# Whole TensorE tiles for the last block of tokens, and a new order of work, in a kernel of linear attention followed by a mixture of attention experts

## The chip, the cores and the metric

The kernel runs on one core of a Trainium2 chip. The metric is device time in microseconds of one execution of the whole program. A core has a matrix engine (TensorE, PE; its weight loads are shown apart as PEld), a vector engine (VectorE, DVE), an activation engine (ScalarE, ACT), a general engine (GpSimd, POOL) and a queue that issues the transfers (SyncE, SP). Each works through its own instructions in the order in which the program gives them and waits for the others by semaphores. PE writes into PSUM, small banks that DVE or ACT empty into SBUF.

## The reference

B = 8 batches of S = 576 tokens, 8 heads of 64 (D = 512), E = 4 experts of width 64, the best 2 of 4 per token. All inputs are f32.

```python
kv  = einsum('bhsd,bhse->bhde', k, v)          # linear attention
out = einsum('bhsd,bhde->bhse', q, kv)
x   = out / sqrt(mean(out * out, -1) + 1e-06) * g_norm
logits = x @ w_gate                            # the best 2 of 4 experts, softmax weights w
for e in range(E):                             # causal attention in each expert
    qe, ke, ve = x @ wq[e], x @ wk[e], x @ wv[e]
    a  = softmax(causal(qe @ ke.T / 8))
    ye = a @ ve @ wo[e]
    result += (e chosen by the token) * w_e * ye
```

## The kernel before

**Tiling.** 576 tokens are cut into NB = 5 blocks: four of 128 and one of REM = 64. D = 512 is cut into NCH = 4 chunks of 128 rows. The four experts go as EP = 2 pairs, two experts side by side on the 128 partitions.

**Steps of one batch, b.** `lk`, `lv`, `lr`, `lq` load k, v, the last 64 tokens of both, and q. `kv` (L409) makes the 64x64 products per head. `q` (L437) transposes q block by block on PE, `qc` (L440) copies it to the tile qT. `out` (L474) multiplies each block of qT by the k-v tile, to which the gate's logits are appended; `oc`, `sq`, `red` copy, square and sum; `nw` is a Newton iteration for the inverse root on DVE; `xm` scales on GpSimd into an x tile (a pool of six, which the stages of the weights share). `x` and `xc` (L560, L563) transpose it to xT. `m8` to `gate` make the expert weights. `v` (L611), `qp` and `kp` (L629) project. For each pair: `sc` (L654) makes five pieces of transposed scores, `exp` (L668) writes them as bf16 into PT, in which key block kb has a strip of the queries from kb's first token on (576, 448, 320, 192 and 64 wide), `msk` masks the diagonal on GpSimd. `pv` (L686) multiplies PT by v with a column of ones: bank 0 holds query blocks 0 to 2 (12 matmuls), bank 1 blocks 3 and 4 (18). `rc`, `iv`, `oc2` (L713 to L726) take the inverse of the ones' column, multiply it by the gate and scale. They read blocks 0 to 2 together, then block 3, then block 4, which has 64 rows. `ot` (L733) transposes five blocks, `otc` copies them to OT, `y` (L743) multiplies by wo, `yc` and `st` copy and store.

**Where block 4 is short.** In `out`, `v`, `y` its stationary operand has 64 columns; in `pv` the stationary operand of query block 4 has 64 columns, and for key block 4 it has 64 rows as well; in `ot` the input has 64 rows. The profile writes the part of PE that is used as rows*columns: 128*128, 128*64, 64*64, 64*128. The `kv` step uses 128*64 by design, two heads beside one another, and the transposes of block 4 of q and x are 64*128.

**Order.** `graph` (L22) lists every step with its engine, its time on the engine, a latency, its needs and the buffers that it holds. `urgency` (L161) gives each a due time from the tables OFFSET, STEP, SECOND (pair 1 against pair 0) and PERIOD (one batch against the next). `plan` (L176) walks through time and always starts the step that can start first, of equals the one due first. The order found is the program's order on every engine, the SP queue's among them. A step that waits holds up all behind it on its engine. The pools' sizes are in POOLS (L142): qT 1, xT 2, PT 3, OT 2, sm and bg (PSUM) 2 and 3, x 6.

Of the kernel before, what the change touches and what calls it, by code (L numbers as in the profile page):

```python
# [21 lines left out]
def graph(B):  # L22
# [18 lines left out]
    for b in range(B):  # L41
        for p in R4 if b == 0 else R2:
            w = 1.0 if b == 0 else 2.0
            tl = (("k", b), ("v", b))
            add(("lk", b, p), "SP", 0.5, 0.45 * w, [("kv", b - 2, c) for c in R4] if p == 0 else [], tl[:1])
            add(("lv", b, p), "SP", 0.5, 0.45 * w, [("kv", b - 2, c) for c in R4] if p == 0 else [], tl[1:])
            if p == 0:
                add(("lr", b), "SP", 1.2, 1.2, [("kv", b - 2, c) for c in R4])
        for i in R5:
            add(("lq", b, i), "SP", 1.1, 1.2 if i < NF else 0.6, [], (("q", b),))  # L50
        if b == 0:
            add(("lg0",), "SP", 2.5, 0.2)
# [22 lines left out]
        for i in R5:  # L75
            pe(("out", b, i), 0.93, [("qc", b, i), ("kvx", b), ("kgc", b)], (("bg", "out", b, i), ("qT", b)))
# [28 lines left out]
        for i in R5:  # L105
            pe(("v", b, i), 0.47, [("xc", b, i), ("ws", "v", 0), ("ws", "v", 1)], (("sm", "v", b, i), ("xT", b)))
            dve(("vc", b, i), 0.43, [("v", b, i)] + [("pv", b - 2, p, g) for p in R2 for g in R2], (("sm", "v", b, i),))
        for p in R2:
            for nm in "qk":
                pe((nm + "p", b, p), 1.06, xT + [("ws", nm, 0), ("ws", nm, 1)], (("bg", nm, b, p), ("xT", b)))  # L110
# [15 lines left out]
            for g in range(3):
                nd = [("pv", b, p, min(g, 1)), ("gate", b)]
                tl = (("bg", "pv", b, p), ("osc", b, p), ("gate", b))
                dve(("rc", b, p, g), 0.17, nd[:1], tl[:2])
                dve(("iv", b, p, g), 0.17, [("rc", b, p, g), ("gate", b)], tl[1:])  # L130
                dve(("oc2", b, p, g), 0.56 if g == 0 else 0.29, [("iv", b, p, g)], tl[:2])
            pe(("ot", b, p), 0.28, [("oc2", b, p, g) for g in range(3)], (("sm", "ot", b, p), ("osc", b, p)))
            act(("otc", b, p), 0.64, [("ot", b, p)], (("sm", "ot", b, p), ("OT", b)))
        for i in R5:
            pe(("y", b, i), 0.45, [("otc", b, 0), ("otc", b, 1), ("wo", "o", 0), ("wo", "o", 1)], (("sm", "y", b, i), ("OT", b)))
# [5 lines left out]
NF = 4  # L141
POOLS = {  # L142
    "k": 2, "v": 2, "q": 2, "sm": 2, "bg": 3, "qT": 1, "kvT": 2, "gl": 2, "x": 6, "xT": 2, "gate": 2,
    "qTp": 3, "PT": 3, "osc": 2, "inv": 2, "OT": 2, "y": 4,
}
PERIOD = 25.7
OFFSET = dict(
    lk=-101.2, lv=-101.2, lr=-101.2, lq=-86.0, lg0=-200, wg=-60, lw=-35.8, ws=-10.8, lwo=-85, wo=-30,
    kv=-61.6, kvx=-60.6, kvc=-60.6, q=-57.9, qc=-75.4, kt=-138.5, ktc=-138.5, kg=-137.5, kgc=-137.5,
    out=-27.6, oc=112.9, sq=29.9, red=-136.3, nw=93.2, gl=94.2, lg=95.2, xm=24.8, x=-29.3, xc=-80.7,  # L150
    m8=19.2, sh=19.2, ex=19.2, mk=19.2, gt=19.2, den=19.2, rd=19.2, gate=19.2, v=2.0, vc=-91.6, qp=40.7,
    qpc=12.5, kp=35.4, kpc=7.2, sc=-1.2, exp=-49.5, msk=4.3, pv=-109.0, rc=-99.4, iv=-99.4, oc2=-99.4,
    ot=13.9, otc=13.9, y=26.5, yc=-17.4, st=26.5,
)
# [21 lines left out]
def plan(tasks, pools, prio):  # L176
# [15 lines left out]
    while len(order) < len(tasks):  # L192
# [42 lines left out]
def kernel(  # L235
# [74 lines left out]
    nc.gpsimd.memset(zrow[:], 0.0)  # L310
    for j in range(2):
# [4 lines left out]
        nc.gpsimd.memset(t[:, :, :, Hd : Hd + 1], 1.0)  # L316
        vexts.append(t)
# [156 lines left out]
    def out_mm(b, i):  # L474
        t0, nt = blocks[i]
# [135 lines left out]
    def v_mm(b, i):  # L611
        t0, nt = blocks[i]
# [16 lines left out]
    def proj(nm, b, pr):  # L629
        p_p = big(nm, b, pr)  # L630
        for c in range(NCH):
            for s in range(2):
# [3 lines left out]
                    rhs=tiles["xT", b][:, c, s * HALF : (s + 1) * HALF],  # L636
# [31 lines left out]
    def exp(b, pr, j):  # L668
        PT = buf(("PT", b, pr), [P, 2, strips], BF16, "PT")
# [132 lines left out]
```

## Time and profile before

| | us |
|---|---|
| median of 3 runs (lowest, highest) | 285.91 (283.67, 286.38) |
| profiled execution | 285.5 |
| its span, first to last instruction | 283.4 |
| PE busy, share of the span | 252.3, 89% |
| DVE busy | 184.7, 65% |
| ACT busy | 160.0, 56% |
| POOL busy | 76.5, 27% |

Busy time is the union of an engine's instructions. Matmuls are pipelined, and an instruction's duration contains time in which the next one runs already; what a group costs in a busy stretch is read from its start to the start of the next group. The granted clock is the share of TensorE's full speed that a stretch had.

### The profile page before, as it was taken

What the parts mean: (1) busy time and instruction counts of PE and PEld (TensorE: products, weight loads), DVE (VectorE), ACT (ScalarE), POOL (GpSimd) and SP (SyncE); (2) the same over time, 40 slices, a digit from 0 to 9 for tenths busy, and PEclk for the clock granted to TensorE, in tenths of its full rate; (3) what the DMA queues carried; (4) which work ended last, traced back from release to release, by engine and by line L of the source; (5) the groups of instructions that cost most, each with busy time, mean ns of one, the idle gap of its engine ahead of it and who ended that gap; (6) DMA issues with size and microseconds to landing.
All of it is one profiled execution on the core that took longest, in us unless ns stands there. A gap on an engine that the chain in (4) does not pass through costs nothing.

```text
span 283.4 us, 6610 instructions
## 1 busy us (share of the span) xinstructions
PE 252.3 (89%) x2576; PEld 219.6 (77%) x2576; DVE 184.7 (65%) x554; ACT 160.0 (56%) x281; POOL 76.5 (27%) x146
## 2 busy tenths in 40 slices
PE   0479768898999797999999999899999999999984
PEld 0469667687898686899889988798889987888850
DVE  1436885988979886266877588857695788215140
ACT  0021203545365568548673977277757777895953
POOL 7000032107107108302072205420271018211210
PEclk9999968999999999799999999999999999999997
DMA  1999998999899951089325962000210111031224
GB/s 42 299 253 307 170 252 217 205 273 262 280 197 230 271 169 56 2 244 222 109 95 130 293 156 85 11 2 37 81 54 0 39 74 58 0 114 57 72 97 168
DMA packets 75551, 40.28 MB, mean 142 GB/s; under 512 B 54272, under 2 KB 70656, under 8 KB 75520
## 3 DMA queue, kind: packets, MB, share of 16 engines
q1 hardware_dynamic: 75520, 39.86, 55.1%
q8 instruction: 20, 0.33, 0.5%
q14 instruction: 11, 0.09, 0.1%
HBM read 30.42 MB, written 9.44 MB: 141 GB/s over the span
## 4 chain that ended last, share of the span: by engine, by line
PE 70%; DVE 14%; DMA 6%; SPq 5%; ACT 2%; issue 2%; ACTq 0%; DVEq 0%
PE p_out L478 12%; PE p_sc L659 9%; PE p_pv L695 7%; PE p_y L747 7%; PE p_k L633 6%; PE p_v L615 6%; PE p_q L633 6%; PE p_q L433 5%; PE p_kv L415 5%; PE p_x L433 4%; SPq L352 3%; DMA w_stage<-in_moe_wq_dram 2%; DMA w_stage<-in_moe_wv_dram 2%; DVE inv L719 2%; DVE mk L588 2%; DVE osc L726 2%
## 5 line engine op out<-in xcount | busy, mean ns | idle before, releaser
L679 POOL TENSOR_SCALAR_AFFINE_SELECT PT<-PT 128x256 bf16<-128x256 bf16 (+1 forms) x80 | 30.1, 387 | 153.1 <-ACT PT L673 139.5
L673 ACT ACTIVATE PT<-p_sc 128x576 bf16<-128x576 f32 (+3 forms) x80 | 51.6, 711 | 9.0 <-PE p_sc L659 8.7
L553 POOL TENSOR_TENSOR x_tok<-o_sb,rs 128x512 f32<-128x512 f32 (+1 forms) x40 | 41.8, 1061 | 40.7 <-DVE rs L529 33.1
L478 PE MATMUL p_out<-kvx,qT 128*128 128x136 f32 (+1 forms) x320 | 47.8, 298 | 1.8 <-DVE qT L443 0.9
L478 PEld LDWEIGHTS p_out<-kvx,qT 128*128 128x128 f32 (+1 forms) x320 | 42.6, 194 | 3.7 <-DVE qT L443 1.1
L659 PE MATMUL p_sc<-qTp,kT 128*128 128x288 f32 (+2 forms) x192 | 39.2, 325 | 0.5 <-ACT PT L673 0.5
L488 DVE COPY o_sb<-p_out 128x544 f32<-128x544 f32 (+1 forms) x40 | 28.4, 717 | 16.9 <-PE p_out L478 15.5
L494 ACT ACTIVATE sq<-o_sb 128x512 f32<-128x512 f32 (+1 forms) x40 | 25.3, 635 | 21.5 <-DVE o_sb L488 20.1
L659 PEld LDWEIGHTS p_sc<-qTp,kT 128*128 128x128 f32 x192 | 28.8, 195 | 5.4 <-issue 1.6
L415 PE MATMUL p_kv<-v_b,k_b 128*64 128x64 f32 x512 | 22.7, 238 | 9.9 <-DMA k_b<-in_k_dram 9.6
L415 PEld LDWEIGHTS p_kv<-v_b,k_b 128*64 128x64 f32 x512 | 19.5, 149 | 12.1 <-DMA v_b<-in_v_dram 9.5
L443 DVE COPY qT<-p_q 128x512 f32<-128x512 f32 (+1 forms) x40 | 25.1, 635 | 5.4 <-PE p_q L433 4.5
L566 ACT CAST xT<-p_x 128x512 fp32r<-128x512 f32 (+1 forms) x40 | 21.4, 544 | 12.7 <-PE p_x L433 12.4
L500 DVE TENSOR_REDUCE ms<-sq 128x8 f32<-128x520 f32 (+1 forms) x40 | 27.2, 685 | 1.8 <-ACT sq L494 1.3
L695 PE MATMUL p_pv<-vext,PT 128*128 128x65 bf16 (+2 forms) x480 | 25.8, 196 | 3.0 <-DVE osc L726 3.0
L695 PEld LDWEIGHTS <-PT 128*128 128x128 bf16 (+2 forms) x480 | 21.5, 101 | 8.8 <-issue 3.1
L754 ACT COPY y<-p_y 128x512 f32<-128x512 f32 (+1 forms) x40 | 23.1, 595 | 9.1 <-PE p_y L747 6.9
L615 PE MATMUL p_v<-wv_r,xT 128*128 128x256 f32 (+1 forms) x160 | 26.2, 293 | 1.3 <-DVE wv_r L395 0.8
L625 DVE CAST vext<-p_v 128x256 bf16<-128x256 f32 (+1 forms) x40 | 16.7, 420 | 16.2 <-PE p_v L615 16.0
L433 PE MATMUL p_q<-ident_f,q_b 128*128 128x128 f32 (+1 forms) x160 | 25.7, 291 | 1.5 <-ACT xT L566 1.2
L648 ACT CAST kT<-p_k 64x576 fp32r<-64x576 f32 x32 | 20.3, 635 | 11.1 <-PE p_k L633 10.9
L747 PE MATMUL p_y<-wo_b,OT 128*128 128x512 bf16 (+1 forms) x80 | 25.0, 405 | 0.5 <-ACT OT L741 0.4
(67 smaller groups left out, 348.3 us busy)
## 6 DMA issues: line engine op xcount, KB each, us to landing
q_b<-in_q_dram SPq DMA_DIRECT2D x32, 256.0 KB, 5.6
out_dram<-y SPq DMA_DIRECT2D x32, 256.0 KB, 2.0
v_b<-in_v_dram SPq DMA_DIRECT2D x14, 512.0 KB, 7.4
k_b<-in_k_dram SPq DMA_DIRECT2D x14, 512.0 KB, 6.3
v_b<-in_v_dram SPq DMA_DIRECT2D x4, 256.0 KB, 4.2
k_b<-in_k_dram SPq DMA_DIRECT2D x4, 256.0 KB, 4.4
k_rem<-in_k_dram SPq DMA_DIRECT2D x8, 128.0 KB, 6.3
v_rem<-in_v_dram SPq DMA_DIRECT2D x8, 128.0 KB, 6.5
```

The costliest lines, as they stand in the source:

```text
L415: nc.tensor.matmul(p_kv[hh * Dh : (hh + 1) * Dh, c, :], lhsT=lhs, rhs=rhs, start=(j == 0), stop=(j == NF), skip_group_check=True,)
L433: nc.tensor.transpose(p_t[:, c, :nt], src[:nt, 2 * c : 2 * c + 2, :].rearrange("p h d -> p (h d)"), ident_f[:nt, :nt])
L478: nc.tensor.matmul(p_o[:nt, c // 2, (c % 2) * 2 * GW : (c % 2 + 1) * 2 * GW], lhsT=tiles["qT", b][:, c, t0 : t0 + nt], rhs=kvx[b % 2][:, c ...
L488: nc.vector.tensor_copy(out=ob[:nt, i].rearrange("p (k h) g -> p k (h g)", k=2), in_=big("out", b, i)[:nt, :, 0 : 4 * GW])
L553: nc.gpsimd.tensor_tensor(out=buf(("x", b, i), [P, H, Dh], FP32, "x_tok")[:nt], in0=ob[:nt, i, :, 0:Dh], in1=st["rstd", b][:nt, i * H : (i ...
L615: nc.tensor.matmul(p_v[:nt, :], lhsT=tiles["xT", b][:, c, t0 : t0 + nt], rhs=w_r["v"][:, c, :, :].rearrange("p e f -> p (e f)"), start=(c ...
L633: nc.tensor.matmul(p_p[:, s, 0:HALF], lhsT=w_r[nm][:, c, 2 * pr : 2 * pr + 2, :].rearrange("p e f -> p (e f)"), rhs=tiles["xT", b][:, c, s ...
L659: nc.tensor.matmul(p_s[:, el, o : o + hi - lo], lhsT=kTs[pr][el][:, kb * P : (kb + 1) * P], rhs=tiles["qTp", b, pr][:, lo:hi], start=True, ...
L673: nc.scalar.activation(PT[:, :, d0 : d0 + o], big("sc", b, pr, j)[:, :, 0:o], ACTF.Exp, scale=scale)
L679: nc.gpsimd.affine_select(out=d, in_=d, compare_op=AluOpType.is_ge, fill=0.0, base=0, pattern=[[0, 2], [1, w]], channel_multiplier=-1,)
L695: nc.tensor.matmul(p_O[:nq, bank, (2 * n + el) * (Hd + 1) : (2 * n + el + 1) * (Hd + 1)], lhsT=PT[:nk, el, col : col + nq], rhs=vexts[b % ...
L747: nc.tensor.matmul(p_y[:nq, :], lhsT=tiles["OT", b][:, pr, s0 : s0 + nq], rhs=wo_b[:, pr, :], start=(pr == 0), stop=(pr == EP - 1),)
```

## The change

The whole last block is made 128 wide. qT, xT, PT and OT, until now buffers from pools, become constant tiles with 64 more columns at the end, set to zero once: one qT, two xT and OT, three PT. In them chunk c's block 4 is read 128 wide, so it reaches over the first 64 tokens of the next chunk or strip; the 64 output rows that come of it are never stored. The rows of v that block 4 lacks are set to zero, its column of ones too. So `out`, `v`, `pv`, `ot` and `y` work on 128*128 tiles throughout; the transposes of block 4 of q and x and the `kv` step stay as they are. With all rows present, `rc`, `iv`, `oc2` read blocks 3 and 4 together: two reads a pair where there were three. One exponential of a column of zeros is put ahead of everything on ACT.

In the planner the needs that the pools expressed are written out, the times of many steps are set anew, the SP queue's latency too, and all of OFFSET, STEP, SECOND and PERIOD. Among the due times, the q, k and v weights (`lw`) move from -35.8 to -50.6, ahead of k and v of batch 2 (2 x 25.4 - 101.1 = -50.3); and the two transfers of wo (-82) come behind the first q block of batch 0 where they came behind the third.

```diff
-            add(("lk", b, p), "SP", 0.5, 0.45 * w, [("kv", b - 2, c) for c in R4] if p == 0 else [], tl[:1])
+            add(("lk", b, p), "SP", 0.5, 0.5 * w, [("kv", b - 2, c) for c in R4] if p == 0 else [], tl[:1])
...
-            add(("lq", b, i), "SP", 1.1, 1.2 if i < NF else 0.6, [], (("q", b),))
+            add(("lq", b, i), "SP", 0.7, 1.35 if i < NF else 0.7, [], (("q", b),))
...
-                    add(("lw", nm, p), "SP", 1.0, 1.3, (), (("x", nm, p),))
+                    add(("lw", nm, p), "SP", 1.0, 1.5, (), (("x", nm, p),))
...
-            pe(("kv", b, c), 0.88, [("lk", b, piece), ("lv", b, piece), ("lr", b)], (("sm", "kv", b), ("k", b), ("v", b)))
+            pe(("kv", b, c), 0.82, [("lk", b, piece), ("lv", b, piece), ("lr", b)], (("sm", "kv", b), ("k", b), ("v", b)))
...
+                ("qc", b, i), 0.42 if last else 0.69, [("q", b, i), ("out", b - 1, i), ("out", b - 1, NF)],
...
-            pe(("out", b, i), 0.93, [("qc", b, i), ("kvx", b), ("kgc", b)], (("bg", "out", b, i), ("qT", b)))
+            pe(
+                ("out", b, i), 0.95, [("qc", b, i), ("qc", b, 0), ("kvx", b), ("kgc", b)],
+                (("bg", "out", b, i),),
+            )
...
+                [("x", b, i)] + [("v", b - 2, j) for j in R5] + [(m, b - 2, p) for m in ("qp", "kp") for p in R2],
...
-            hold = (0.25, 0.25, 0.39, 0.28, 0.29)
+            hold = (0.27, 0.27, 0.43, 0.33, 0.45)
...
+            old = [("pv", n // 2, n % 2, g) for g in R2]
...
+                act(("exp", b, p, j), took[j], [("sc", b, p, j)] + old, (("bg", "sc", b, p, j),))
...
-            for g in range(3):
+            for g in R2:
...
-PERIOD = 25.7
+PERIOD = 25.4
 OFFSET = dict(
-    lk=-101.2, lv=-101.2, lr=-101.2, lq=-86.0, lg0=-200, wg=-60, lw=-35.8, ws=-10.8, lwo=-85, wo=-30,
-    kv=-61.6, kvx=-60.6, kvc=-60.6, q=-57.9, qc=-75.4, kt=-138.5, ktc=-138.5, kg=-137.5, kgc=-137.5,
-    out=-27.6, oc=112.9, sq=29.9, red=-136.3, nw=93.2, gl=94.2, lg=95.2, xm=24.8, x=-29.3, xc=-80.7,
+    lk=-101.1, lv=-101.1, lr=-101.1, lq=-83.0, lg0=-200, wg=-60, lw=-50.6, ws=-25.6, lwo=-85, wo=-30,
+    kv=-61.7, kvx=-60.7, kvc=-60.7, q=-60.4, qc=-50.3, kt=-108.9, ktc=-108.9, kg=-107.9, kgc=-107.9,
+    out=-44.7, oc=31.8, sq=45.8, red=-155.3, nw=62.4, gl=63.4, lg=64.4, xm=93.6, x=-27.6, xc=-100.1,
...
-    x=1.5, xc=2.0, out=1.9, oc=1.9, sq=1.9, red=1.9, v=0.9, vc=0.5, y=1.7, yc=2.0, st=1.6, lq=1.5,
+    x=0.4, xc=0.4, out=1.4, oc=1.4, sq=1.5, red=1.4, v=0.9, vc=1.0, y=1.1, yc=1.1, st=1.1, lq=1.8,
...
-SECOND = 9.2
+SECOND = 15.6
...
+    warm = const.tile([P, 1], FP32, name="warm")
+    nc.scalar.activation(warm[:], zrow[:, 0:1], ACTF.Exp)
+
+    PAD = NB * P - S
+    qT = const.tile([P, NCH * S + PAD], FP32, name="qT")
+    nc.gpsimd.memset(qT[:, NCH * S :], 0.0)
...
+        t = const.tile([P, NCH * S + PAD], FP32R, name=f"xT{j}")
+        nc.vector.tensor_copy(out=t[:, NCH * S :], in_=zrow[:, 0:PAD])
...
+        t = const.tile([P, 2, strips + PAD], BF16, name=f"PT{j}")
+        nc.gpsimd.memset(t[:, :, strips:], 0.0)
...
+    def blocks_of(t, c):
+
+        return t[:, c * S : c * S + NB * P]
...
+        nc.gpsimd.memset(t[REM:P, NF], 0.0)
         vexts.append(t)
...
-                p_o[:nt, c // 2, (c % 2) * 2 * GW : (c % 2 + 1) * 2 * GW],
-                lhsT=tiles["qT", b][:, c, t0 : t0 + nt],
+                p_o[:, c // 2, (c % 2) * 2 * GW : (c % 2 + 1) * 2 * GW],
+                lhsT=blocks_of(qT, c)[:, i * P : (i + 1) * P],
...
-                p_v[:nt, :],
-                lhsT=tiles["xT", b][:, c, t0 : t0 + nt],
+                p_v[:],
+                lhsT=blocks_of(xTs[b % 2], c)[:, i * P : (i + 1) * P],
...
-                    nk = blocks[kb][1]
-                    col = strip_off[kb] + s0 - kb * P
+                    col = strip_off[kb] + (qc - kb) * P
                     nc.tensor.matmul(
-                        p_O[:nq, bank, (2 * n + el) * (Hd + 1) : (2 * n + el + 1) * (Hd + 1)],
-                        lhsT=PT[:nk, el, col : col + nq],
-                        rhs=vexts[b % 2][:nk, kb, 2 * pr + el, :],
+                        p_O[:, bank, (2 * n + el) * (Hd + 1) : (2 * n + el + 1) * (Hd + 1)],
+                        lhsT=PT[:, el, col : col + P],
+                        rhs=vexts[b % 2][:, kb, 2 * pr + el, :],
...
-    PARTS = ((0, 0, 3), (3, 1, 1), (4, 1, 1))
...
-                p_t[:, s0 : s0 + nq], tiles["osc", b, pr][:nq, qc, :, :].rearrange("p e f -> p (e f)"), ident_b[:nq, :nq]
+                p_t[:, qc * P : (qc + 1) * P], tiles["osc", b, pr][:, qc, :, :].rearrange("p e f -> p (e f)"), ident_b[:]
...
-                p_y[:nq, :], lhsT=tiles["OT", b][:, pr, s0 : s0 + nq], rhs=wo_b[:, pr, :],
+                p_y[:], lhsT=blocks_of(OTs[b % 2], pr)[:, qc * P : (qc + 1) * P], rhs=wo_b[:, pr, :],
```

## Rows read from the trace of the kernel before

**Rows 1.** The page: span, then busy us (share) and instructions of each engine

```profile
span 283.4 us, 6610 instructions
PE 252.3 (89%) x2576; PEld 219.6 (77%) x2576; DVE 184.7 (65%) x554; ACT 160.0 (56%) x281; POOL 76.5 (27%) x146
```

**Rows 2.** Stretches: length, PE, PEld, DVE, ACT, POOL busy (instructions), PE clock, DMA share, GB/s

```profile
22.00:35.00 13.00, 11.86 (x136) 10.88 (x134) 9.81 (x20) 3.16 (x5) 0.00 (x0) 1.00 1.04 241
35.00:68.00 33.00, 26.63 (x241) 23.91 (x242) 26.02 (x78) 12.01 (x22) 7.94 (x10) 0.90 1.01 246
68.00:130.00 62.00, 57.85 (x622) 51.18 (x621) 46.83 (x137) 37.22 (x67) 21.15 (x34) 0.97 0.76 183
130.00:265.00 135.00, 133.26 (x1379) 118.07 (x1378) 90.88 (x285) 95.25 (x168) 39.91 (x72) 1.00 0.29 81
```

**Rows 3.** Timeline of PE around P@V: start, us, engine, line, operation, form, count

```profile
203.30 1.54 PE L695 MATMUL p_pv<-vext,PT 128*128 128x65 bf16 x30
204.78 0.62 PE L747 MATMUL p_y<-wo_b,OT 128*64 128x512 bf16 x2
...
209.21 0.54 PE L695 MATMUL p_pv<-vext,PT 128*128 128x65 bf16 x12
209.68 0.69 PE L415 MATMUL p_kv<-v_b,k_b 128*64 128x64 f32 x16
...
210.95 1.18 PE L695 MATMUL p_pv<-vext,PT 128*128 128x65 bf16 x18
212.06 1.32 PE L633 MATMUL p_q<-xT,wq_r 128*128 128x288 f32 x8
```

**Rows 4.** The same timeline around v, y, ot and out

```profile
201.38 1.11 PE L615 MATMUL p_v<-wv_r,xT 128*128 128x256 f32 x8
202.33 0.69 PE L659 MATMUL p_sc<-qTp,kT 128*128 128x288 f32 x4
202.86 0.60 PE L747 MATMUL p_y<-wo_b,OT 128*128 128x512 bf16 x2
...
205.32 0.97 PE L659 MATMUL p_sc<-qTp,kT 128*128 128x448 f32 x4
...
218.90 0.52 PE L736 MATMUL p_ot<-ident_b,osc 128*128 128x128 bf16 x5
219.35 1.19 PE L478 MATMUL p_out<-kvx,qT 128*128 128x136 f32 x8
...
220.81 1.09 PE L478 MATMUL p_out<-kvx,qT 128*128 128x136 f32 x8
221.74 0.60 PE L433 MATMUL p_x<-ident_f,x_tok 128*128 128x128 f32 x4
...
225.86 1.14 PE L478 MATMUL p_out<-kvx,qT 128*64 128x136 f32 x8
226.94 0.61 PE L747 MATMUL p_y<-wo_b,OT 128*128 128x512 bf16 x2
```

**Rows 5.** Weight loads by line and form: count, busy us, mean ns, idle before

```profile
L478 PEld LDWEIGHTS p_out<-kvx,qT 128*128 128x128 f32 x256 | 35.5, 209 | 1.8 <-DVE osc L726 0.9 <-PE p_out L478 0.4
L695 PEld LDWEIGHTS <-PT 128*128 128x128 bf16 x320 | 11.8, 97 | 5.9 <-issue 3.1 <-POOL PT L679 0.8
L478 PEld LDWEIGHTS p_out<-kvx,qT 128*64 128x64 f32 x64 | 7.1, 136 | 1.9 <-DVE qT L443 1.1 <-issue 0.4
```

**Rows 6.** Chain that ended last, in order of time: start, us, what

```profile
17.50 1.28 ACT L427
...
58.98 5.69 DMA w_stage<-in_moe_wv_dram
...
140.65 1.04 PE p_k L633 x8
...
170.11 1.04 PE p_k L633 x8
```

**Rows 7.** Timeline of the SP queue: start, us, line, transfer, count

```profile
40.92 5.00 SPq L392 DMA_DIRECT2D w_stage<-in_moe_wq_dram  x4
```

More of the change, by code (lines that the diff above doesn't have):

```diff
@@ L215, in plan @@
         if eng == "SP":
-            dma = max(dma, t + hold + 1.3) + lat
-            fin = dma + 0.5
+            dma = max(dma, t + hold + 1.6) + lat
+            fin = dma + 0.6
         end = max(end, fin)
@@ L310, with tokens @@
     nc.gpsimd.memset(zrow[:], 0.0)
+    warm = const.tile([P, 1], FP32, name="warm")
[3 more added lines that the diff above has]
+    nc.gpsimd.memset(qT[:, NCH * S :], 0.0)
+    xTs, PTs, OTs = [], [], []
+    for j in range(2):
+        t = const.tile([P, NCH * S + PAD], FP32R, name=f"xT{j}")
+        nc.vector.tensor_copy(out=t[:, NCH * S :], in_=zrow[:, 0:PAD])
+        xTs.append(t)
+        t = const.tile([P, EP * S + PAD], BF16, name=f"OT{j}")
+        nc.gpsimd.memset(t[:, EP * S :], 0.0)
+        OTs.append(t)
+    for j in range(3):
+        t = const.tile([P, 2, strips + PAD], BF16, name=f"PT{j}")
+        nc.gpsimd.memset(t[:, :, strips:], 0.0)
+        PTs.append(t)
+    def blocks_of(t, c):
+        return t[:, c * S : c * S + NB * P]
+    def tokens(t, i):
+        t0, nt = blocks[i]
+        return t[:, 0 : (t.shape[1] - PAD)].rearrange("p (c s) -> p c s", s=S)[:, :, t0 : t0 + nt]
     for j in range(2):
@@ L440, in q_copy @@
     def q_copy(b, i):
-        t0, nt = blocks[i]
-        qT = buf(("qT", b), [P, NCH, S], FP32, "qT")
-        nc.vector.tensor_copy(out=qT[:, :, t0 : t0 + nt], in_=small(None, "q", b, i)[:, :, :nt])
+        nt = blocks[i][1]
+        nc.vector.tensor_copy(out=tokens(qT, i), in_=small(None, "q", b, i)[:, :, :nt])
     def kt(b):
@@ L474, in out_mm @@
     def out_mm(b, i):
-        t0, nt = blocks[i]
         p_o = big("out", b, i)
@@ L563, in x_copy @@
     def x_copy(b, i):
-        t0, nt = blocks[i]
-        xT = buf(("xT", b), [P, NCH, S], FP32R, "xT")
-        nc.scalar.copy(xT[:, :, t0 : t0 + nt], small(None, "x", b, i)[:, :, :nt])
+        nt = blocks[i][1]
+        nc.scalar.copy(tokens(xTs[b % 2], i), small(None, "x", b, i)[:, :, :nt])
     def small_t(b, name, shape):
@@ L635, in proj @@
                     lhsT=w_r[nm][:, c, 2 * pr : 2 * pr + 2, :].rearrange("p e f -> p (e f)"),
-                    rhs=tiles["xT", b][:, c, s * HALF : (s + 1) * HALF],
+                    rhs=blocks_of(xTs[b % 2], c)[:, s * HALF : (s + 1) * HALF],
                     start=(c == 0),
@@ L677, in msk @@
             w = blocks[kb][1]
-            d = tiles["PT", b, pr][:w, :, strip_off[kb] : strip_off[kb] + w]
+            d = PTs[(2 * b + pr) % 3][:w, :, strip_off[kb] : strip_off[kb] + w]
             nc.gpsimd.affine_select(
@@ L701, in pv @@
                     )
-    PARTS = ((0, 0, 3), (3, 1, 1), (4, 1, 1))
     def part(b, pr, g):
-        qc, bank, n = PARTS[g]
-        nq = blocks[qc][1]
-        o = (qc - GROUPS[bank][1][0]) * 2 * (Hd + 1)
-        po = big("pv", b, pr)[:nq, bank, o : o + n * 2 * (Hd + 1)].rearrange("p (n f) -> p n f", f=Hd + 1)
-        iv = buf(("inv", b, pr), [P, NB, 2], FP32, "inv")[:nq, qc : qc + n, :]
-        return qc, n, nq, po, iv
+        bank, qcs = GROUPS[g]
+        qc, n = qcs[0], len(qcs)
+        po = big("pv", b, pr)[:, bank, 0 : n * 2 * (Hd + 1)].rearrange("p (n f) -> p n f", f=Hd + 1)
+        iv = buf(("inv", b, pr), [P, NB, 2], FP32, "inv")[:, qc : qc + n, :]
+        return qc, n, po, iv
     def rc(b, pr, g):
-        _, _, _, po, iv = part(b, pr, g)
+        _, _, po, iv = part(b, pr, g)
         nc.vector.reciprocal(iv.rearrange("p n e -> p (n e)").unsqueeze(2), po[:, :, Hd : Hd + 1])
     def ivm(b, pr, g):
-        qc, n, nq, _, iv = part(b, pr, g)
+        qc, n, _, iv = part(b, pr, g)
         nc.vector.tensor_tensor(
-            out=iv, in0=iv, in1=tiles["gate", b][:nq, qc : qc + n, 2 * pr : 2 * pr + 2], op=AluOpType.mult
+            out=iv, in0=iv, in1=tiles["gate", b][:, qc : qc + n, 2 * pr : 2 * pr + 2], op=AluOpType.mult
         )
     def o_scale(b, pr, g):
-        qc, n, nq, po, iv = part(b, pr, g)
+        qc, n, po, iv = part(b, pr, g)
         osc = buf(("osc", b, pr), [P, NB, 2, Hd], BF16, "osc")
         nc.vector.tensor_tensor(
-            out=osc[:nq, qc : qc + n, :, :].rearrange("p n e f -> p (n e) f"),
+            out=osc[:, qc : qc + n, :, :].rearrange("p n e f -> p (n e) f"),
             in0=po[:, :, 0:Hd],
-            in1=iv.rearrange("p n e -> p (n e)").unsqueeze(2).to_broadcast([nq, 2 * n, Hd]),
+            in1=iv.rearrange("p n e -> p (n e)").unsqueeze(2).to_broadcast([P, 2 * n, Hd]),
             op=AluOpType.mult,
@@ L733, in ot @@
     def ot(b, pr):
-        p_t = small([P, S], "ot", b, pr, dtype=BF16)
-        for qc, (s0, nq) in enumerate(blocks):
+        p_t = small([P, NB * P], "ot", b, pr, dtype=BF16)
+        for qc in range(NB):
             nc.tensor.transpose(
-                p_t[:, s0 : s0 + nq], tiles["osc", b, pr][:nq, qc, :, :].rearrange("p e f -> p (e f)"), ident_b[:nq, :nq]
+                p_t[:, qc * P : (qc + 1) * P], tiles["osc", b, pr][:, qc, :, :].rearrange("p e f -> p (e f)"), ident_b[:]
             )
     def ot_copy(b, pr):
-        nc.scalar.copy(buf(("OT", b), [P, EP, S], BF16, "OT")[:, pr, :], small(None, "ot", b, pr)[:])
+        nc.scalar.copy(OTs[b % 2][:, pr * S : (pr + 1) * S], small(None, "ot", b, pr)[:, 0:S])
     def y_mm(b, qc):
-        s0, nq = blocks[qc]
         p_y = small([P, D], "y", b, qc)
```

65 lines of the change are left out of this document (33 added, 32 removed).

## The prediction

> **What bounds the kernel now.** I first read the page's totals [rows 1], then the busy time by stretch [rows 2], because a share over the whole span mixes a start that waits for data with a middle that doesn't. In [rows 1] the reader sees TensorE (PE) at 252.3 of 283.4 us. In [rows 2] it divides: from 130 to 265 us PE is busy 133.26 of 135 us at full clock, while VectorE (DVE) has 90.88 and ScalarE (ACT) 95.25, and the DMA engines 29%. From 35 to 68 us it is otherwise: the DMA share is 1.01, PE has 26.63 of 33, and its clock is 0.90. So there are two regimes: a start limited by transfers and by the first batch's chain of dependent steps, and some 200 us in which PE alone sets the pace. PE's missing time from 68 to 265 us is 4.15 + 1.74 = 5.9 us in all. What shortens PE's stream there shortens the kernel, unless it opens waits.
>
> A busy PE is not yet a useful PE, so next comes the timeline of PE in one repeated stretch [rows 3], read by starts: from the start of one group to the start of the next is what the group costs. Twelve P@V matmuls, all on 128*128 tiles, take from 209.21 to 209.68, 0.47 us, and the next group (p_kv) is on another tile size. The eighteen of bank 1 take from 210.95 to 212.06, 1.11 us. These contain query block 4, whose matmuls go 128*64 four times, 64*64 once, and again for the second expert: four changes of tile size inside and one on leaving. With a spacing s in an unbroken run and a price c of a change, 12s + c = 0.47 and 18s + 5c = 1.11; so c = 0.116 us and s = 0.0295 us. The thirty from 203.30 to 204.78 test it: 30s + 5c = 1.47 against 1.48 measured. Over half of bank 1's time is changes of tile size.
>
> **The change, part by part.**
>
> P@V. Each of the 16 (batch, pair) calls has its five changes taken away, since every operand is a 128*128 tile afterwards: 5c = 0.58 us where a 128*128 group follows, 4c = 0.46 where the next group is of another size anyway. I take 0.55: 16 x 0.55 = 8.8 us. Bounds: if the whole-tile matmuls run at 0.47/12 = 0.039, eighteen take 0.70 and the gain is 0.41, 6.6 us in all; at the most 16 x 0.58 = 9.3.
>
> Output transposes (16 calls). Five take from 218.90 to 219.35, 0.45 us [rows 4], with one change in and one out, 2c = 0.23. The last transpose becomes twice as wide, so I take 0.17 (between c and 2c): 2.7 us, bounds 1.9 and 3.7.
>
> Output product of the attention (out, 8 calls of block 4). A full block takes 220.81 to 221.74, 0.93; the 64-token block 225.86 to 226.94, 1.08. Gain 0.15 x 8 = 1.2. y: the 64-token block takes 204.78 to 205.32, 0.54 [rows 3, 4], a full one 202.86 to 203.30, 0.44: 0.10 x 8 = 0.8. v: a full and the last block together take 201.38 to 202.33, 0.95; the kernel's own table has 0.47 for a full one, so the last costs nothing extra: 0, at most 16c = 1.9.
>
> Sum on PE: 8.8 + 2.7 + 1.2 + 0.8 = 13.5 us, bounds 10.5 and 16.9.
>
> What it adds to PE is wider weight loads: 34 a batch go from 64 to 128 columns (20 in P@V, 8 in out, 4 in v, 2 in y). I cost them at nothing: the 128-column P load lasts 97 ns [rows 5], yet its matmuls stand 29.5 ns apart, so loads lie under one another; in out the load does grow, from 136 to 209 ns, but the block with the short loads is the slower one [rows 4]. If that cover were gone, 73 ns each is 34 x 8 x 0.073 = 19.9 us. The Trainium skill speaks against the change here: "TensorE: Matmul & The Clock Gate", section LDWEIGHTS, has the time of a load grow with its columns, at 1.2 a nanosecond, whatever the rows. By that 64 more columns would be an estimated 53 ns, 34 x 8 x 0.053 = 14.5 us, which would eat the whole sum on PE. The f32 rows agree that a load grows; the P@V rows disagree on the figure, since 128 columns of P take 97 ns and lie under matmuls that start every 29.5 ns.
>
> DVE. The normalisation of blocks 3 and 4 becomes one read: three instructions fewer a pair, 48 in all. From 130 to 265 us DVE has 44 us free [rows 2], so I cost it at 0; it can only help, by tenths of a microsecond, where nothing covers it, at the end of the kernel.
>
> Fixed tiles. qT, xT, PT and OT become constant tiles with explicit needs. The first q copy of a batch waited for the end of the previous batch's out (qT had one buffer) and still waits for its block 4; xT and OT alternate over two, PT over three, as their pools did. Behind a waiting copy stands all of DVE or ACT, but the events are the same ones: 0. Eight more memsets on GpSimd and two copies on DVE stand ahead of the loop; GpSimd is idle from 22 to 35 us [rows 2], so 0.
>
> The early exponential moves the table load of 1.28 us out from between the k-v copy and its transpose [rows 6]. That sits in the chain that ended last, but the next 17 us are full of transfers (DMA share 1.04 from 22 to 35 us). Between 0 and 1.28, I take 0.5.
>
> Loads. By the new due times the SP queue sends the q-weights (four transfers) before k and v of batch 2, and k- and v-weights (eight) right after these; so far the first goes at 40.92 [rows 7], the v-weights behind q of batch 2, and the chain of waits holds 5.69 us of a v-weight's transfer, up to 64.67 [rows 6]. They move past those k, v and rest transfers (q-weights) and five q transfers (v-weights). Gain: at the most what PE lacks from 35 to 68 us, 6.4. Loss: batch 2's k and v come later by 512 KB at 246 GB/s, 2.1 us. The two wo transfers move ahead of q blocks 1 and 2 of batch 0, the same 512 KB, but those q copies feed a chain that stands for k and v of batch 1 next. The six stages of weights also fill the six x buffers, so the first x tiles still wait for weights. Both ends are far apart; I take a gain of 1.0.
>
> New waits. Every due time is changed, and the planner's table now charges PE more: its PE costs of one batch, added up, were 27.1 us and are 28.1 now, while PE really needs 29.5 (from one k projection at 140.65 to the same of the next batch at 170.11 [rows 6]) less 13.5/8, 27.8. So far PE ran later than planned and found its inputs ready; now plan and PE agree, and small delays show. From 68 to 130 us, where PE isn't saturated, it lacks 6.7% [rows 2]; if 130 to 265 became like that, 9.0 us would be missing instead of 1.7, 7.3 more. Between 0 and 7.3, I take 2.5, nearer to the saturated rows.
>
> Sum: the profiled execution took 285.5 us (span 283.4, 2.1 around it), the median of the runs is 285.91. 285.5 - 13.5 - 0.5 - 1.0 + 2.5 = 273.0.
>
> **Rivals.**
>
> B, the freed time turns into waits: PE stops being the bound and the middle runs as 68 to 130 does. For it: the re-made order. Against: DVE and ACT have some 30% free from 130 to 265 us. Time: 285.5 - 13.5 - 1.5 + 7.3 = 277.8.
>
> C, the wider loads bind (other side): the 73 ns of the f32 loads are paid by PE in all 34 loads a batch. Time: 285.5 - 13.5 - 1.5 + 19.9 = 290.4; it is slower by over 1% once 17.9 of the 19.9 us stay uncovered. Against it: the 29.5 ns spacing. By the figure of the Trainium skill (the same page and section) C would give an estimated 285.5 - 15.0 + 14.5 = 285.0.
>
> D, the new order starves PE (other side): in-order PE stands before a group whose input is planned too early, over the whole middle. From 35 to 68 us it lacks 19%; at that rate 197 us lose 38, 32 more than now: 302. It decides from 17.9 us of extra waits, 12% of the stretch. Against: the 30% that DVE and ACT have free.
>
> E, the tile changes cost nothing: bank 1 is slow because its masks come late. Then 285.5 - 1.5 = 284. Against: the thirty and the eighteen fit one c, in different places.
>
> **How the numbers follow.** Forecast 0.63; still faster (weights and v at their upper bounds) 0.03; B 0.17; E 0.08; D 0.06; C 0.03. The likeliest is 273.0. Forecast and B hold 0.80; their bounds (PE's sum at its ends, startup up to 4 better, waits of up to 7.3) give 266 to 282. Faster by over 1% (about what a measurement of this kernel can tell from no change) is 0.63 + 0.03 + 0.17 = 0.83; within 1% is E, 0.08; slower is C and D, 0.09.
>
> **What would show it.** Eighteen P@V matmuls of bank 1 start-to-start in about 0.55 us, thirty in about 0.9, and no 64-wide form at that line; out's last block at 0.93; PE busy lower by 12 to 15 us; the table load before 10 us; the last v-weight landed before 58 us; PE's missing time from 68 us to the last batch between 6 and 13 us. I am wrong if whole-tile P@V matmuls stand further apart than 0.04 us (C), if bank 1 keeps 1.1 us (E), or if PE's waits in the middle grow beyond 13 us (B, D).

## The result, and the profile after

| | before | after |
|---|---|---|
| median of the runs, us (lowest to highest) | 284.79 (282.77 to 286.38) | 270.58 (270.32 to 270.85) |
| profiled execution, its span | 285.5, 283.4 | 270.39, 268.7 |
| PE busy | 252.3 | 234.8 |
| span less PE busy | 31.1 | 33.9 |
| DVE, ACT busy | 184.7, 160.0 | 180.8, 159.3 |

The ratio of after to before is 0.9505, 95% interval 0.9433 to 0.9577: 14.2 us faster. The forecast was 273.0 with a range of 266 to 282. A single run that took over 1.5% longer than the fastest of its kernel (in a5_late_weights, a8_reversed_ties, b1_old_order_whole_tiles and b2_before_reversed_ties) is left out of every median below.

The page of the changed kernel, its totals (answering [rows 1]):

```profile
span 268.7 us, 6606 instructions
PE 234.8 (87%) x2562; PEld 209.5 (78%) x2576; DVE 180.8 (67%) x508; ACT 159.3 (59%) x282; POOL 77.1 (29%) x154
```

PE is busy 17.5 us less and the span is 14.7 us shorter: some of what PE saved came back as time in which it is not busy. The stretches, with the columns of [rows 2]:

```profile
22.00:35.00 13.00, 11.67 (x140) 10.67 (x139) 10.76 (x22) 3.53 (x6) 0.00 (x0) 0.88 1.11 250
35.00:68.00 33.00, 29.99 (x291) 26.91 (x292) 28.82 (x83) 15.04 (x30) 12.03 (x15) 1.00 1.09 244
68.00:130.00 62.00, 58.27 (x654) 53.99 (x656) 48.48 (x132) 39.70 (x71) 17.57 (x30) 0.97 0.87 205
130.00:250.00 120.00, 116.48 (x1317) 105.54 (x1326) 82.90 (x247) 88.78 (x157) 38.62 (x70) 1.00 0.27 80
```

From 35 to 68 us PE is now busy 29.99 us instead of 26.63. From 130 us on it was all but saturated before (1.74 missing in 135 us); now 3.52 are missing in 120. The timeline of PE around P@V and the output transposes, answering [rows 3, 4]:

```profile
199.97 0.72 PE L727 MATMUL p_pv<-vext,PT 128*128 128x65 bf16 x18
200.53 0.60 PE L495 MATMUL p_kg<-wg_bd,kvT 128*128 128x16 f32 x4
...
206.22 0.44 PE L765 MATMUL p_ot<-ident_b,osc 128*128 128x128 bf16 x5
206.50 1.15 PE L514 MATMUL p_out<-kvx,qT 128*128 128x136 f32 x8
...
217.14 1.08 PE L727 MATMUL p_pv<-vext,PT 128*128 128x65 bf16 x30
218.06 1.03 PE L775 MATMUL p_y<-wo_b,OT 128*128 128x512 bf16 x3
```

The eighteen matmuls of bank 1 go from start to start of the next group in 0.56 us (1.11 before), the thirty in 0.92 (1.48), the five transposes in 0.28 (0.45). So in these groups the tiles do what the prediction said. Whether they made the whole difference is what the experiments had to tell, since the order of work had changed with them.

### The profile page after: what moved, and what is told of

Read it like the earlier page. It is cut to its first block, busy times and chain, and to the rows that moved or that the text cites. A ratio compares the mean times of both kernels' runs of the same rounds, so it can differ in the third digit from the quotient of the medians.

```text
span 268.7 us, 6606 instructions
## 1 busy us (share of the span) xinstructions
PE 234.8 (87%) x2562; PEld 209.5 (78%) x2576; DVE 180.8 (67%) x508; ACT 159.3 (59%) x282; POOL 77.1 (29%) x154
## 4 chain that ended last, share of the span: by engine, by line
PE 60%; SPq 15%; DVE 14%; ACT 3%; DMA 2%; issue 2%; POOL 1%; POOLq 0%; ACTq 0%; DVEq 0%
PE p_out L514 11%; PE p_sc L693 8%; PE p_v L649 7%; PE p_q L667 6%; PE p_pv L727 5%; SPq L407 5%; PE p_y L775 5%; PE p_x L471 5%; PE p_q L471 5%; PE p_k L667 5%; SPq L390 4%; DMA w_stage<-in_moe_wk_dram 2%; DVE osc L755 2%; SPq L430 2%; DVE gt L629 2%
## 5 line engine op out<-in xcount | busy, mean ns | idle before, releaser
L514 PE MATMUL p_out<-kvx,qT 128*128 128x136 f32 x320 | 45.3, 287 | 0.4 <-DVE o_sb L524 0.2
L514 PEld LDWEIGHTS p_out<-kvx,qT 128*128 128x128 f32 x320 | 41.0, 194 | 1.6 <-DVE o_sb L524 0.4
L453 PE MATMUL p_kv<-v_b,k_b 128*64 128x64 f32 x512 | 22.3, 236 | 13.5 <-DMA k_b<-in_k_dram 12.2
L693 PEld LDWEIGHTS p_sc<-qTp,kT 128*128 128x128 f32 x192 | 28.2, 190 | 4.2 <-DVE osc L755 0.9
L782 ACT COPY y<-p_y 128x512 f32<-128x512 f32 (+1 forms) x40 | 22.5, 584 | 9.2 <-PE p_v L649 4.1
L536 DVE TENSOR_REDUCE ms<-sq 128x8 f32<-128x520 f32 (+1 forms) x40 | 26.5, 681 | 0.8 <-ACT sq L530 0.8
L471 PE MATMUL p_q<-ident_f,q_b 128*128 128x128 f32 (+1 forms) x160 | 24.0, 276 | 3.3 <-DVE qT L480 2.2
L649 PE MATMUL p_v<-wv_r,xT 128*128 128x256 f32 x160 | 25.8, 293 | 0.0
L682 ACT CAST kT<-p_k 64x576 fp32r<-64x576 f32 x32 | 20.3, 633 | 4.0 <-PE p_k L667 3.5
L471 PE MATMUL p_x<-ident_f,x_tok 128*128 128x128 f32 (+1 forms) x160 | 22.1, 268 | 0.5 <-POOL x_tok L589 0.5
L775 PE MATMUL p_y<-wo_b,OT 128*128 128x512 bf16 x66 | 21.5, 406 | 1.0 <-ACT OT L770 0.7
L471 PEld LDWEIGHTS p_q<-ident_f,q_b 128*128 128x128 f32 (+1 forms) x160 | 18.1, 146 | 5.6 <-DVE qT L480 2.6
```

The source lines that it names most:

```text
L453: nc.tensor.matmul(p_kv[hh * Dh : (hh + 1) * Dh, c, :], lhsT=lhs, rhs=rhs, start=(j == 0), stop=(j == NF), skip_group_check=True,)
L471: nc.tensor.transpose(p_t[:, c, :nt], src[:nt, 2 * c : 2 * c + 2, :].rearrange("p h d -> p (h d)"), ident_f[:nt, :nt])
L514: nc.tensor.matmul(p_o[:, c // 2, (c % 2) * 2 * GW : (c % 2 + 1) * 2 * GW], lhsT=blocks_of(qT, c)[:, i * P : (i + 1) * P], rhs=kvx[b % 2][ ...
L536: nc.vector.tensor_reduce(mss[b % 2][:nt, i, :], sqs[(NB * b + i) % 3][:nt], axis=AX_X, op=AluOpType.add)
L649: nc.tensor.matmul(p_v[:], lhsT=blocks_of(xTs[b % 2], c)[:, i * P : (i + 1) * P], rhs=w_r["v"][:, c, :, :].rearrange("p e f -> p (e f)"), ...
L693: nc.tensor.matmul(p_s[:, el, o : o + hi - lo], lhsT=kTs[pr][el][:, kb * P : (kb + 1) * P], rhs=tiles["qTp", b, pr][:, lo:hi], start=True, ...
```

## Experiments

**An order for equals.** In `plan`, of the steps that can start together the one due first is taken; several steps are due at the same time (the k, v and rest transfers of a batch, the five `xm` of a batch), and they stand in Python sets, whose order the program does not fix. So the order among equals is open, and with it everything planned behind it. To compare kernels that share one order, the variants below have one rule for equals.

```diff
-        t, _, _, n = min(((t, p, e, n) for t, p, e, n in starts if e == eng and t <= t0 + 0.02), key=lambda x: x[1])
+        t, _, _, n = min(((t, p, e, n) for t, p, e, n in starts if e == eng and t <= t0 + 0.02), key=lambda x: (x[1], x[3]))
```

> The changed kernel, with one edit in its planner: of steps that can start together and are due together, the one whose name comes first is taken; until now such ties were left open. All the variants below have the same rule, so that they share one order of work on every engine. If ties matter little, it takes what the changed kernel took, 270.6 us within 1%; if the order among equals (the k and v transfers at the start above all) matters, it lies up to some 3 us off.

It took 262.97 us (262.54 to 264.81), 7.6 less than the changed kernel, whose tiles, costs and due times it has. That is outside what I had expected (up to some 3 us): equals matter far more. Its totals, and the row of the granted clock in 40 slices:

```profile
span 261.6 us, 6644 instructions
PE 229.5 (88%) x2576; PEld 206.7 (79%) x2576; DVE 178.4 (68%) x508; ACT 159.4 (61%) x282; POOL 77.5 (30%) x154
PEclk9999899999999999999999999999999999999999
```

The same row of the changed kernel:

```profile
PEclk9997999999997999999999999999999999999967
```

PE is busy 5.3 us less for the same matmuls, and the mean granted clock is 0.993 where it was 0.973. The changed kernel's clock falls three times, once in the middle. There its timeline of PE, with the wait and what ended it in brackets, has

```profile
82.64 0.46 PE L471 MATMUL p_q<-ident_f,q_b 64*128 64x64 f32 x4 [2.21 <-DVE qT L480]
83.03 2.10 PE L667 MATMUL p_q<-xT,wq_r 128*128 128x288 f32 x8
```

and its stretches

```profile
80.00:83.00 3.00, 0.80 (x8) 0.52 (x6) 3.00 (x5) 1.37 (x3) 2.96 (x5) 1.00 1.19 142
83.00:87.00 4.00, 4.00 (x35) 3.83 (x34) 1.58 (x9) 0.64 (x1) 0.00 (x0) 0.57 1.05 211
```

PE stood for 2.21 us behind a q copy; then eight matmuls of the q projection took 2.10 us, where the same eight take 1.31 under the rule for equals (second fence below), and the granted clock from 83 to 87 us was 0.57, most of it at the lower of the two levels. With the rule for equals the same stretches read

```profile
80.00:83.00 3.00, 2.01 (x15) 1.68 (x15) 2.95 (x11) 0.86 (x2) 1.08 (x2) 1.00 0.96 218
83.00:87.00 4.00, 4.00 (x35) 3.61 (x33) 2.07 (x6) 3.79 (x7) 1.31 (x4) 1.00 0.87 185
```

PE is busy 2.01 of the 3 us, and the clock stays at 1.00. Its timeline shows the eight at full clock:

```profile
75.94 1.31 PE L667 MATMUL p_q<-xT,wq_r 128*128 128x288 f32 x8
77.09 1.23 PE L667 MATMUL p_k<-xT,wk_r 128*128 128x288 f32 x8
```

**The rule turned round.** Of equals the last name first.

```diff
+    rank = {n: i for i, n in enumerate(sorted(tasks, key=repr, reverse=True))}
...
-  key=lambda x: (x[1], x[3]))
+  key=lambda x: (x[1], rank[x[3]]))
```

(of the last two lines only the end is shown)

> a0_fixed_ties with the rule for ties turned round: of steps that can start together and are due together, the last name first. No cost, due time or tile differs. If a0_fixed_ties is so far below the changed kernel (263.0 against 270.6) by a particular order among equals, this one lies elsewhere, some 263 to 273 us; if any fixed rule does, it lies within 1% of 263.0.

269.08 us (268.74 to 269.16). So no rule is good in itself: three orders among equals gave the changed kernel 270.6, 263.0 and 269.1.

**The kernel before with the same two rules.** The edits are those just shown.

> The kernel before with the same rule for ties as a0_fixed_ties. Within 1% of the kernel before, 284.8 us, if ties matter little; its distance to a0_fixed_ties is then the change at one rule for ties.

> b0_before_fixed_ties with the rule for ties turned round. If the order among equals is a matter of chance for the kernel before as well, it lies somewhere from 282 to 292 us; and whichever it is, the distance to a8_reversed_ties is the change at this rule. My account of tiles and order together, from the runs so far: 14 to 28 us above a8_reversed_ties.

289.36 us (288.14 to 290.47) and 287.36 (287.35 to 290.36), against 283.31 and 283.69 for the kernel before, measured beside them. At one rule for equals the change is worth 26.4 and 18.3 us, not 14.2. The open order that was measured as before was the best of its three, the one measured as after the worst of its three.

**Three reads instead of two.** The normalisation of blocks 3 and 4 is divided again, on whole tiles.

```diff
-        _, _, po, iv = part(b, pr, g)
-        nc.vector.reciprocal(...)
+        for h in (0,) if g == 0 else (1, 2):
+            _, _, _, po, iv = part(b, pr, h)
+            nc.vector.reciprocal(...)
```

(and the same in `ivm` and `o_scale`)

> As a0_fixed_ties, but blocks 3 and 4 of P@V are read in two instructions each time where the change reads them in one: 48 DVE instructions more, the tiles stay whole. My account, by which DVE is covered by PE: 0 to 0.5 us slower. If instead the merged read was a main source of the gain (DVE on the path from P@V to the output transposes), 3 us or more slower, 16 times about 0.2 us.

262.24 us (261.75 to 262.89); ratios to before 0.924 (0.9188 to 0.9293) and 0.9271 (0.9216 to 0.9325): no difference that can be told. The merged read was worth nothing.

**The short tiles back, in the same order.** Every engine's instructions stand as in a4_three_reads; only the sizes of the last block's tiles differ.

```diff
-                        lhsT=PT[:, el, col : col + P],
-                        rhs=vexts[b % 2][:, kb, 2 * pr + el, :],
+                        lhsT=PT[:nk, el, col : col + nq],
+                        rhs=vexts[b % 2][:nk, kb, 2 * pr + el, :],
...
-                lhsT=blocks_of(qT, c)[:, i * P : (i + 1) * P],
+                lhsT=blocks_of(qT, c)[:, i * P : i * P + blocks[i][1]],
```

(and likewise ot, v and y; in the second run P@V and ot alone)

> As a4_three_reads, but P@V, the output transposes, out, v and y have their short last block back (128*64, 64*64 and 64*128 tiles), in the same order of work. My account, a price of 0.116 us for each change of tile size: 13.5 us slower than a4_three_reads (10.5 to 16.9), PE busy 12 to 17 us more. The rival that gives the gain to the new order of work and the new due times: under 4 us slower.

> As a1_all_short, but only P@V and the output transposes have the short last block; out, v and y are on whole tiles. My account: 8.8 + 2.7 = 11.5 us slower than a4_three_reads (8.5 to 13.0), so out, v and y together are worth 2.0 (2.0 to 3.9). The rival of the order: under 3 us slower.

270.66 us (269.58 to 271.85) with all short, 268.61 (268.04 to 269.05) with P@V and ot short. The totals of a4_three_reads,

```profile
span 260.0 us, 6692 instructions
PE 229.6 (88%) x2576; PEld 206.5 (79%) x2576; DVE 178.3 (69%) x556; ACT 159.5 (61%) x282; POOL 77.5 (30%) x154
```

of a1_all_short

```profile
span 267.9 us, 6693 instructions
PE 242.7 (91%) x2576; PEld 210.8 (79%) x2576; DVE 175.8 (66%) x556; ACT 160.9 (60%) x282; POOL 77.7 (29%) x154
```

and of a2_pv_ot_short

```profile
PE 241.9 (91%) x2576; PEld 214.9 (81%) x2576; DVE 178.0 (67%) x556; ACT 159.5 (60%) x282; POOL 77.7 (29%) x154
```

Whole tiles take 13.1 us of work off PE (242.7 to 229.6) and 8.4 us off the time (270.66 to 262.24): the time outside PE's work grows from 25.2 to 30.4 us. P@V and ot are 12.3 us of the work and 6.4 of the time; out, v and y add 2.05 to the time. PE's work came out as expected, but both times are misses: I had expected 13.5 (10.5 to 16.9) and 11.5 (8.5 to 13.0).

The three profiles differ in their clocks (1.00, 0.985 and 0.991), so the split of the work is not fair as it stands. If each stretch of PE's busy time is multiplied by its granted clock, an estimate, the work is 242.7 us with all short, 238.5 with P@V and ot short and 228.0 with none. From one matmul to the next the tile size changes 213, 171 and 63 times in these traces. So out, v and y are 4.2 us for 42 changes, P@V and ot 10.5 for 108: 0.10 us a change in both.

**Changes of tile size without narrow loads.** Key block 4 alone goes by 64 rows; all loads keep 128 columns.

```diff
+                    nk = blocks[kb][1]
...
-                        lhsT=PT[:, el, col : col + P],
-                        rhs=vexts[b % 2][:, kb, 2 * pr + el, :],
+                        lhsT=PT[:nk, el, col : col + P],
+                        rhs=vexts[b % 2][:nk, kb, 2 * pr + el, :],
```

> As a0_fixed_ties, but the matmuls of key block 4 against query block 4 use 64 rows (tile 64*128) and everything else stays 128*128: two such matmuls a pair, so four changes of tile size a pair where there are none; all loads keep 128 columns. If a change costs 0.116 us: 16 x 4 x 0.116 = 7.4 us slower than a0_fixed_ties. If what cost time in the kernel before was the narrow loads or the narrow output (64 columns), and not the change: 0 to 1 us slower.

Its totals, and the thirty matmuls of one P@V in its timeline:

```profile
span 263.0 us, 6629 instructions
PE 236.5 (90%) x2561; PEld 211.5 (80%) x2576; DVE 176.9 (67%) x508; ACT 159.5 (61%) x282; POOL 77.6 (30%) x154
```

```profile
214.78 1.39 PE L728 MATMUL p_pv<-vext,PT 128*128 128x65 bf16 x30
216.10 1.04 PE L776 MATMUL p_y<-wo_b,OT 128*128 128x512 bf16 x3
```

The thirty take 1.32 us where all-whole ones take 0.92: 0.40 for four changes, 0.10 each. PE's work grows by 7.0 us (229.5 to 236.5), 0.109 for each of the 64 changes, with no narrow load anywhere: what costs is the change. That it is not the 64-row matmul itself is seen from its starts: in P@V of this trace a matmul starts 0.029 us after the one before it where the tile stays 128*128, 0.125 after it on going to 64*128 and 0.133 on coming back (medians). The time grows by only 2.3 us (265.30 against 262.97), where I had expected 7.4, a miss; between the two profiles the time in which PE isn't busy falls from 32.1 to 26.5 us, so most of the added work went into time in which PE had waited anyway.

**Whole tiles in the old order.** Tiles, constant buffers and the early exponential of the change; graph, costs, due times and three reads of before.

```diff
-<graph, POOLS, PERIOD, OFFSET, STEP, SECOND, plan of after>
+<those of before, with the rule for equals>
```

> Whole tiles, constant buffers and the early exponential of the changed kernel, but the planner's table, needs, due times and three reads of the kernel before (rule for ties as in a0_fixed_ties): the change of tiles without the change of order. My account: 13.5 us less than b0_before_fixed_ties (10.5 to 16.9) and up to 1.3 for the table load, less the waits that open, 0 to 7.3; so 8 to 15 us faster, some 271 to 275 us. If the gain came from the new due times: under 4 us faster.

282.57 us (280.05 to 283.75), 6.8 less than b0_before_fixed_ties and 20.3 more than a4_three_reads, which has the same instructions in the new order. I had expected 8 to 15 us less, so this too is a miss.

```profile
span 282.0 us, 6705 instructions
PE 240.6 (85%) x2561; PEld 214.5 (76%) x2576; DVE 182.4 (65%) x556; ACT 158.9 (56%) x282; POOL 77.8 (28%) x154
PEclk9999995999999998699999999799988999999997
```

The order takes 11.0 us off PE's busy time (240.6 to 229.6) and 11.0 off the rest of the span (41.4 to 30.4). The first of these is nearly all the clock: the slices show five falls, the mean is 0.957 against 0.991, and PE's busy time multiplied by its granted clock is an estimated 229.6 and 228.0 us. The number of changes of tile size is much the same (57 and 63).

**The old due times alone.** New tiles, costs, latencies and needs; OFFSET, STEP, SECOND and PERIOD of before.

> a0_fixed_ties with OFFSET, STEP, SECOND and PERIOD of the kernel before; the planner's costs, latencies and needs, the whole tiles and the merged read are those of the change. If the order is worth 20 us (b1_old_order_whole_tiles against a4_three_reads) by the new due times: 275 to 284 us. If by the new costs and latencies, with which the plan fits the engines' real times: 262 to 268 us.

277.82 us (275.88 to 278.65), 14.9 more than a0_fixed_ties. That is twice what the rule for equals moves (7.6), so I ascribe most of the order's gain to the due times; that is an inference, as each plan also has its own order among equals. What remains to b1_old_order_whole_tiles, 4.8, is within that spread, and open.

**Late weights.** The due times of the weights as before. In the queue this moves the q-weights alone: the v-weights still go ahead of q of batch 2, where they went behind it in the kernel before.

```diff
-lw=-50.6, ws=-25.6
+lw=-35.8, ws=-10.8
```

(these two entries of OFFSET)

> a0_fixed_ties with the due times of the weights as before (-35.8, and -10.8 for their scaling): the q-weights go behind k and v of batch 2 again, the other two where they were. My account: 1.0 us slower at the most, and up to 2.1 us faster, since k and v of batch 2 come sooner by 512 KB. The rival that the earlier weights shorten the start: 2 to 6 us slower.

271.47 us (268.58 to 271.71), 8.5 more than a0_fixed_ties, far outside my account (1.0 slower at the most) and beyond the rival's 2 to 6. The profiled run is the fastest of them, 268.58. Its stretch from 35 to 68 us, and DVE's first scaling of a weight:

```profile
35.00:68.00 33.00, 28.32 (x294) 25.93 (x293) 25.41 (x77) 11.58 (x21) 10.29 (x13) 0.95 1.07 248
```

```profile
47.22 0.48 DVE L433 TENSOR_SCALAR wq_r<-w_stage,g_wide 128x512 fp32r<-128x512 f32 x1 [5.95 <-DMA w_stage<-in_moe_wq_dram]
```

and the same with the early weights:

```profile
35.00:68.00 33.00, 31.01 (x308) 28.93 (x309) 30.06 (x88) 17.94 (x34) 12.01 (x15) 1.00 1.07 244
```

```profile
38.53 0.48 DVE L433 TENSOR_SCALAR wq_r<-w_stage,g_wide 128x512 fp32r<-128x512 f32 x1
```

All of DVE stood 5.95 us behind the scaling of a weight that had not landed, and PE did 2.7 us less in that stretch. That much I put down to the weights. The rest of the 8.5 lies elsewhere, and a due time that moves anything moves what is planned behind it; neither part is separated by a run from the spread of 7.6.

**The k-v product as one step.**

```diff
-            pe(("kv", b, c), 0.82, [("lk", b, piece), ("lv", b, piece), ("lr", b)], ...)
+            pe(("kv", b, 0), 2.6, [(m, b, p) for m in ("lk", "lv") for p in R2] + [("lr", b)], ...)
```

(for batches 1 to 7; all four parts are issued together)

> As a0_fixed_ties, but the k-v product of batches 1 to 7, whose tiles are 128*64, is one step for the planner where it was four, so nothing is put between its parts. In the changed kernel about three groups a batch stand apart, so some four changes of tile size a batch go: 7 x 4 x 0.116 = 3.2 us less on PE. By the price of a change: 1 to 3 us faster than a0_fixed_ties. If the longer step holds up what is due meanwhile, or the order found is a worse one: 0 to 3 us slower.

264.43 us (263.96 to 266.22), 1.5 more than a0_fixed_ties. A miss, and inconclusive. PE's time not busy is no longer than there (31.3 us against 32.1), and the tile size changes 46 times against 63, 17 fewer and not 28. But the mean clock was 0.980 against 0.993: from 252 to 259 us, at the end of the work, it was 0.51, where a0_fixed_ties had 1.00. So what the fewer changes were worth isn't seen in the time.

Not tried: the early exponential by itself, and a version of the planner that looks for the best order among equals. Of all kernels run, a0_fixed_ties and a4_three_reads are the fastest, 7.6 and 8.3 us below the changed kernel.

## Why the prediction was right, and where it was not

**The sum on PE** was 13.5 us with bounds 10.5 and 16.9; at one order it measures 13.1, or an estimated 14.7 with the clock taken out. The price of a change of tile size, 0.116 us from [rows 3], measures 0.109 over 64 changes and 0.10 over the 150 between a1_all_short and a4_three_reads; the spacing, 0.0295 us, is 0.92/30 = 0.031. With the clock taken out, P@V and ot, priced at 11.5, measure 10.5, and out, y and v, priced at 2.0, measure 4.2. What the prices of out and y left out is the change on entering the short block: it falls to the group before, and the prediction read the short block from its own start on. A full block of out takes 0.93 us before another 128*128 group and 1.02 before one of another size (medians of a4_three_reads at full clock); 16 such entries are an estimated 1.5 of the 2.2 us, and the rest, v's share among it, is open.

Of the signs foretold, bank 1 and the thirty came out as said, and out's last block takes 0.84 to 0.93 us in batches 3 to 7; PE's busy time fell by 17.5 us where 12 to 15 were foretold, and between two kernels of unlike order the difference is open.

**The wider loads** were costed at nothing, and PE's work fell by what was foretold, so rival C fell; the loads' own busy time fell too (PEld 210.8 us in a1_all_short, 206.5 in a4_three_reads). With C falls the estimated 14.5 us that the rule on weight loads in the Trainium skill ("TensorE: Matmul & The Clock Gate", section LDWEIGHTS) would have added. Rival E, that the changes cost nothing, fell with a3_key_block_64_rows. Another page of the Trainium skill, "TensorEngine Tiling (Array Packing)", section Tiling Modes, says that changing the tiling mode, and not merely the tile, drains the engine. The trace agrees that a change of mode costs time, 0.10 to 0.11 us here; that it is a drain isn't shown.

**The merged read** was costed at 0 and measures 0. **The table load** stands at 0.81 us as foretold, ahead of everything; its 0.5 us was not measured apart:

```profile
0.81 1.28 ACT L322 ACT_TABLE_LOAD   x1 [0.81 <-PEq L814]
```

**New waits** were put at 2.5 us, between 0 and 7.3. From 68 to 250 us PE lacks 3.73 + 3.52 = 7.3 us, inside the 6 to 13 foretold. But between a1_all_short and a4_three_reads the time outside PE's work grows by 5.2 us as PE's work falls by 13.1. That is the term that was mis-sized: I took a value near the saturated rows, although PE was being relieved of a twentieth of its work. In part, then, rival B came true. So whole tiles are worth 8.4 us in this order and 6.8 in the old one (there with the constant tiles and the early exponential), not 11 (13.5 less 2.5).

**The weights** landed before 58 us as foretold: the last one is scaled at 54.07, where its transfer held the chain to 64.67 before [rows 6].

```profile
54.07 0.48 DVE L433 TENSOR_SCALAR wv_r<-w_stage,g_wide 128x512 fp32r<-128x512 f32 x1
```

Priced at a gain of 1.0, they seem to be worth more: PE did 2.7 us less in that stretch with the q-weights late, though no run separates this from the order that moved with it. I had looked at what arrives late and not at what stands behind it: a scaling on DVE that waits for its transfer holds up every copy behind it.

**The new due times** were in my account only as a source of waits (B, D). This is the step that failed, and its sign was wrong: in an order with one rule for equals they and the new costs are worth 18.7 us (b0_before_fixed_ties to a1_all_short, both on short tiles; the constant tiles and the early exponential are in it), more than the tiles. I came near 270.6 because what I left out cancelled, which is luck: 18.7 gained by the order, and 13.0 lost by the orders among equals that were measured (the kernel before lay 5.4 us below its fixed rule, 283.93 against 289.36, the changed one 7.6 above). Along this chain of runs, 8.4 for tiles and 18.7 for the order, less 13.0 and less 0.7 between a4_three_reads and a0_fixed_ties, is 13.4, the distance from 283.93 to 270.58. Such a chain adds up by its making and doesn't show that the steps are independent: the tiles measure 8.4 in one order and 6.8 in the other. The forecast of the time was right, then, and its reason, the tiles, accounts for 8.4 of the 14.2 us.

## What to carry to other kernels

Price a change of PE's tile size from the starts of two groups that differ in it, and count changes, not sizes: widening the last block to the whole tile removed some 0.10 us for each. Count the change on entering a group as well as the one on leaving it. When one engine is saturated and a twentieth of its work goes, part of that can come back as waits: here it was a third or more, in an order that was planned with the new times. And before two versions of a planned kernel are compared, fix what the planner leaves open: here the order among equals alone was worth 7.6 us, half of the 14.2 that the change was measured to be worth.

## What the runs showed of the hardware

I had not expected how much of a worse order is paid in PE's clock. b1_old_order_whole_tiles and a4_three_reads do the same matmuls; half of the 22.0 us between their spans is PE being busy longer, at mean clocks of 0.957 and 0.991. In the changed kernel a single wait of 2.21 us, with PE busy 0.80 of 3 us, was followed by a stretch granted 0.57; with PE busy 2.01 of the same 3 us the clock stayed at 1.00. So a wait of PE may cost its own length and then some: the eight matmuls behind it took 2.10 us instead of 1.31.

Not every such wait does. In a5_late_weights PE waited 2.68 us and was busy 0.32 of the 3 us from 86 to 89, and from 89 to 93 the clock was 1.00; in a8_reversed_ties it waited 2.63 us, was busy 0.75 of the 3 us from 81 to 84, and the clock from 84 to 88 was 1.00. The row of a5_late_weights has no fall there (a slice is 6.7 us):

```profile
PEclk9999997999999999999999999999999999999998
```

What decides whether the clock falls is open in these runs.
